# Score products head by head, DFT tables copied later, and a reordered start of each Fourier mixing

## The chip, the cores and the metric

One core of one Trainium2 chip runs the whole program. The metric is device time in microseconds (us), taken as the median of several executions. One execution is also profiled; the instruction rows, waits and granted TensorE clock quoted below come from that one. Five engines work side by side, each through its own queue in order: TensorE (PE, with its weight loads in a row called PEld), VectorE (DVE), ScalarE (ACT), GpSimd (POOL), and SyncE (SP), which only issues transfers.

## The reference

There are two blocks. The first is attention with a threshold, for 8 batches of 8 heads, 576 rows and head dimension 64:

```
scores = scale * q @ k^T
thresh = max(scores, -1) - tau
scores = where(scores >= thresh, scores, -1e9)
attn   = softmax(scores)            # denominator + 1e-9
x      = (attn @ v), heads side by side  -> (8, 576, 512)
```

The second mixes that x and puts it through a channel network:

```
mixed = real(fft over 512 of (fft over 576 of x))
u  = x + mixed
un = (u - mean(u)) / sqrt(var(u) + 1e-6)
out = u + relu(un @ w_ch1) @ w_ch2        # 512 -> 2048 -> 512
```

Everything is fp32; the two weight matrices arrive as float64 and are converted on the chip.

## The kernel before, in words

**Steps.** The attention goes in steps `i`, 20 to a batch (`per_batch`). A pair of heads takes five steps: step `t = i % 5` from 0 to 3 handles 128 query rows of both heads, step 4 the last 64 rows of both together. In a step, `scores` multiplies q by k into two PSUM tiles `sc`, one per head, each 576 wide and made in two halves (L434); the two heads lie on different 64 partitions. The softmax takes the negated maximum (`neg`, L455 in the first two batches, L512 after), the exponentials on ACT (L463, L518) together with a threshold (`thr`), and one DVE instruction that masks and sums (L471, L532). That instruction is the last reader of `sc`. Only two `sc` tiles exist, so the scores of the next step wait for it, head by head. `weights_in_parts` transposes the weights of the step before on PE (`pe` L579, `pw` L597) and copies them out on ACT (`ends` L585, `e_t` L599). `values_in_parts` multiplies them by v (`pv`, L628) and copies the result to `x` (DVE L637 in the first two batches, ACT L635 after). The first pair of a batch goes to a tile called `x_first`. PE results other than scores share four PSUM banks (tag `mm`), handed out in order: a bank is written again only when its last reader is done.

**First batch.** Its 20 steps (`step(i)`) carry, beside attention, the conversion of the first weight matrix in 16 chunks: integer and float passes on DVE (L293, L296, L308), ACT, and POOL (L313, L316). Filler products on PE (`busy`, L111) stand where nothing else is to be done. At the end of step 3 POOL copies the channel DFT table out of the staging tile `dim_raw` (`copy_dim`, 26 instructions), at the end of step 4 the sequence DFT table out of `f` (`copy_seq`), and then clears all of `f` (L228). `fold_rows` adds and subtracts mirrored rows of x into `f`; after the second pair, `fold_halves` (L710, L711) forms sums and differences of two of its chunks on POOL.

**Later batches.** From batch 3 on (`late`) the main loop interleaves one batch's attention with the Fourier mixing and the channel network of rows already mixed. `fill()` sets the interleaving: each call adds a fixed share to a budget, may advance the mixing by one piece (`mix(1)`), and issues channel products until the budget is spent. The first products (`ph`, L1192) and second products (`po`, L1379) use a two-level fast matrix scheme, with sums on DVE and POOL. A mixing begins at step 2 of the following batch (`start_batch`). Its first three pieces are only folds of `f` on DVE (L710, L711, L736, L732, L741). The later ones are products: `py` against the channel table (L751) and `pa` against the sequence table (L768, L772). `Rows.factors` makes the inverse standard deviations: a square root on ACT (L866), an exponential to bring the other function table back (L869), then a DVE reciprocal (L870). `Rows.add` (L877) is what uses them.

Nothing is scheduled by the compiler in this part: each engine executes in the order in which the Python code issues (`manual_schedule`).

Of the kernel before, what the change touches and what calls it, by code (L numbers as in the profile page):

```python
# [9 lines left out]
FP32 = mybir.dt.float32  # L10
# [37 lines left out]
def kernel(  # L48
# [12 lines left out]
    nc = tc.nc  # L61
# [157 lines left out]
    def copy_seq():  # L219
        nc.gpsimd.memset(seq_xe[:, :, :], 0.0)  # L220
        nc.gpsimd.memset(seq_xo[:, :, :], 0.0)
        for u, (pieces, dst, parity, parts) in enumerate(SEQ):
            for p, n in parts:
                for c in range(2):
                    nc.gpsimd.tensor_copy(
                        dst[p : p + n, c, :], f[p : p + n, u, KH * c + parity : KH * (c + 1) : 2]
                    )
        nc.gpsimd.memset(f[:, :, :], 0.0)  # L228

    dim_c = const.tile([128, 1 + 256], FP32, name="dim_c")
    dim_s = const.tile([128, 256], FP32, name="dim_s")

    def load_dim():
        raw = sb.tile([128, DM], FP32, tag="tmp", bufs=1, name="dim_raw")
        nc.sync.dma_start(out=raw[:, :], in_=dft_dim[0:128, :])

        nc.sync.dma_start(out=raw[0:1, EH:DM], in_=dft_dim[128:129, EH:DM])  # L240
        return raw

    def copy_dim(raw):
        nc.gpsimd.memset(dim_s[:, 0:1], 0.0)
        nc.gpsimd.tensor_copy(dim_c[:, 0:1], raw[:, 256:257])
        for u, r in enumerate((0, 2, 1, 3)):
            for n, at in ((32, 0), (1, 32), (31, 33)):
                i = 4 * at + r
                f, step = (i, 4) if i <= 128 else (384 - i, -4)
                c = 64 * u + at  # L250
                nc.gpsimd.tensor_copy(dim_c[:, 1 + c : 1 + c + n], _stepped(raw, f, step, n))

                if f == 0:
                    c, f, n = c + 1, f + step, n - 1
                nc.gpsimd.tensor_copy(dim_s[:, c : c + n], _stepped(raw, 256 + f, step, n))

    w1 = [const.tile([128, HID], FP32, name=f"w1_{c}") for c in range(ND)]
# [12 lines left out]

    hs = const.tile([128, NJ * BT], FP32, name="hs")

# [151 lines left out]
    def scores(i):  # L424
# [5 lines left out]
        if t < 4:  # L430
            for c in range(2):
                for j in range(2):
                    hp, k0 = slice(64 * j, 64 * j + 64), D * (1 - j)
                    nc.tensor.matmul(  # L434
                        sc[j][:, c, 0:HALF], qT[hp, 128 * t : 128 * t + 128],
                        kT[hp, k0 + HALF * c : k0 + HALF * (c + 1)], start=True, stop=True,
                    )
        else:
            for c in range(2):
                nc.tensor.matmul(  # L440
                    sc[0][:, c, 0:HALF], q_ends[:, :], kT[:, D + HALF * c : D + HALF * (c + 1)],
                    start=True, stop=True,
                )
        steps[i] = (sc, nh)

    def softmax(i, between=None, meanwhile=None, behind=None):
# [14 lines left out]
        for j in range(nh):  # L461
# [12 lines left out]
            )  # L474
            if between is not None:
                between()
                between = None
        if behind is not None:
            behind()
        den = inverse(i, nh)  # L480
        if normalized(i // NT):
            nc.vector.tensor_scalar(
# [178 lines left out]
    def fold_rows(n):  # L661
# [39 lines left out]

        if n % NPAIR == 1 and b != 1:
            fold_halves(b)
# [127 lines left out]
    class Rows:  # L831
# [32 lines left out]
        def factors(self):  # L864
# [4 lines left out]
            nc.scalar.activation(out=warm[:, :], in_=eps[:, :], func=ACT.Exp)  # L869
            nc.vector.reciprocal(self.rstd[:, :], self.rstd[:, :])  # L870

        def add(self, t, cols, product):

            u = self.us[t][:, cols]
            if len(product.shape) == 3:
# [591 lines left out]

    def fill(hold=False):
        nonlocal budget, spent
        holding[:] = [True] if hold else []  # L1470
        budget += per_slot
        if mixes and not ended and not hold:
            mix(1)
# [14 lines left out]
    def step(i):  # L1488
# [17 lines left out]
        if t == 1 and n > 0:  # L1506
            softmax(i, lambda: weighted_values(n - 1, 1), next_stages, last_stage)
            load_v(n + 1)
        elif t == 3:
            softmax(i, lambda: weighted_values(n, 0), next_stages, last_stage)  # L1510
        else:
            softmax(i, None, next_stages, last_stage)
# [24 lines left out]
        spread_inverse(i)  # L1537
        if i == 3:
            copy_dim(raw)
        if i == 4:  # L1540
            copy_seq()

    folds = []
# [30 lines left out]
    chunks[3] = w1_chunk(3)  # L1574
    raw = load_dim()
    load_seq()
    load_v(1)
    LAST = HID // WC - 1
# [132 lines left out]
    for i in range(2 * per_batch, total):  # L1711
# [8 lines left out]
        elif t == 1 and n > 0:  # L1720
            while folds:
                fold_more()
            values = values_in_parts(n - 1, 1)
        next(values, None)
        if i < total:
            softmax_first(i)
        next(values, None)
        if i % per_batch == 2:
            for _ in last_fold:
# [34 lines left out]
        if i % per_batch == 1:  # L1764
            next(last_fold)
        fill()
        if t == 2 and n + 1 < B * NPAIR:
# [32 lines left out]
    start_batch(B - 1)  # L1800
    for _ in range(3):
        mix(1)
        fill(True)
# [55 lines left out]
```

## Time and profile before

| what | value |
|---|---|
| median of 3 runs | 1591.63 us (1590.78 to 1592.55) |
| the profiled execution | 1591.6 us, its span 1589.8 us |
| busy in the span | PE 1537.3 us (97%), DVE 1054.1 (66%), ACT 917.1 (58%), POOL 777.3 (49%) |
| mean granted TensorE clock | 0.989 |
| 0 to 134 us (about the first batch) | PE busy 120.6 of 134, DVE 106.5, granted clock 0.95 |
| 134 to 290 us (about the second batch) | PE busy 141.9 of 156, DVE 112.2, granted clock 0.99 |
| 485 to 1305 us (four of the later batches) | PE busy 804.4 of 820 |

A row of the timeline gives the start in us, the duration, engine, line, operation, what it writes and reads, how many instructions were merged in it, and in brackets how long the engine sat idle before it and whose end released it. A row of the waits gives who waited for whom: total us, how often, the longest. A row of the windows gives a stretch, the busy time of each engine in it and the TensorE clock granted there as a share of full speed. PE counts as busy while a matmul is in flight, so a PE at a lower clock still looks busy.

### The profile page before, as it was taken

What the parts mean: (1) busy time and instruction counts of PE and PEld (TensorE: products, weight loads), DVE (VectorE), ACT (ScalarE), POOL (GpSimd) and SP (SyncE); (2) the same over time, 40 slices, a digit from 0 to 9 for tenths busy, and PEclk for the clock granted to TensorE, in tenths of its full rate; (3) what the DMA queues carried; (4) which work ended last, traced back from release to release, by engine and by line L of the source; (5) the groups of instructions that cost most, each with busy time, mean ns of one, the idle gap of its engine ahead of it and who ended that gap; (6) DMA issues with size and microseconds to landing.
All of it is one profiled execution on the core that took longest, in us unless ns stands there. A gap on an engine that the chain in (4) does not pass through costs nothing.

```text
span 1589.8 us, 27001 instructions
## 1 busy us (share of the span) xinstructions
PE 1537.3 (97%) x9786; PEld 1189.8 (75%) x9786; DVE 1054.1 (66%) x2119; ACT 917.1 (58%) x1921; POOL 777.3 (49%) x961
## 2 busy tenths in 40 slices
PE   8989989999999999999999999999999999999999
PEld 4556445555788877877787878877787778889999
DVE  6887776845868566666568466756577666655546
ACT  6775776454665566656766566656666666222231
POOL 4772563034455552546254633545264625546735
PEclk9999999999999999999999999999999999999999
DMA  6423331556956254634445344634464434636655
GB/s 164 128 58 116 76 90 23 168 155 195 318 156 214 70 166 122 205 109 142 141 153 164 116 130 134 203 99 143 125 195 133 137 120 154 213 138 233 237 195 184
DMA packets 248907, 239.31 MB, mean 151 GB/s; under 512 B 197027, under 2 KB 218533, under 8 KB 228678
## 3 DMA queue, kind: packets, MB, share of 16 engines
q1 hardware_dynamic: 246262, 237.28, 48.9%
q8 instruction: 78, 1.28, 0.3%
q10 hardware_dynamic: 2512, 0.30, 0.1%
q14 instruction: 55, 0.45, 0.1%
HBM read 205.93 MB, written 31.46 MB: 149 GB/s over the span
## 4 chain that ended last, share of the span: by engine, by line
PE 81%; DVE 10%; ACT 5%; issue 1%; DMA 1%; POOL 0%; SPq 0%; DVEq 0%; ACTq 0%
PE ph L1192 24%; PE po L1379 17%; PE pv L628 10%; PE sc L434 9%; PE pw L597 7%; PE po L915 4%; PE ph L891 2%; PE sc L440 2%; PE py L751 2%; PE pa L768 1%; DVE neg L455 1%; PE pa L772 1%; PE pe L579 1%; ACT e L518 1%; DVE e L471 1%
## 5 line engine op out<-in xcount | busy, mean ns | idle before, releaser
L512 DVE TENSOR_REDUCE neg<-sc 128x1 f32<-128x576 f32 x216 | 154.3, 751 | 140.0 <-PE sc L434 120.6
L518 ACT ACTIVATE e<-sc,neg 128x576 f32<-128x576 f32 x216 | 158.4, 733 | 144.0 <-DVE neg L512 143.6
L1379 PE MATMUL po<-w,w_all 128*128 128x128 f32 x1728 | 220.9, 278 | 0.3 <-ACT ends L585 0.3
L1379 PEld LDWEIGHTS po<-w,w_all 128*128 128x128 f32 x1728 | 206.6, 193 | 9.8 <-issue 7.1
L1129 DVE TENSOR_TENSOR hs<-ph,hs 128x512 f32<-128x512 f32 (+1 forms) x128 | 105.3, 823 | 160.3 <-PE ph L1192 103.6
L1138 POOL TENSOR_TENSOR w<-hs 128x512 f32<-128x512 f32 x32 | 42.0, 1315 | 317.9 <-ACT hs L1134 244.2
L597 PE MATMUL pw<-ident,e 128*128 128x128 f32 x1152 | 171.4, 276 | 12.6 <-ACT x_first L635 9.0
L1192 PE MATMUL ph<-u_t,w 128*128 128x256 f32 x768 | 180.5, 381 | 0.7 <-DMA w<-f 0.6
L532 DVE SCALAR_TENSOR_TENSOR e<-sc,thr,e 128x576 f32<-128x576 f32 x216 | 168.2, 811 | 18.5 <-ACT thr L522 18.5
L434 PE MATMUL sc<-kT,qT 64*128 64x288 f32 x1024 | 168.9, 432 | 11.3 <-DVE e L471 9.4
L599 ACT COPY e_t<-pw 128x512 f32<-128x512 f32 x256 | 148.6, 594 | 46.0 <-PE pw L597 44.5
L541 ACT ACTIVATE e<-e,den 128x576 f32<-128x576 f32 x216 | 157.6, 776 | 8.3 <-DVE den L385 7.6
L1192 PEld LDWEIGHTS ph<-u_t,w 128*128 128x128 f32 x768 | 141.2, 190 | 23.5 <-issue 4.5
L597 PEld LDWEIGHTS pw<-ident,e 128*128 128x128 f32 x1152 | 135.9, 142 | 30.5 <-ACT x_first L635 10.0
L1192 PE MATMUL ph<-w_all,w 128*128 128x256 f32 x672 | 157.1, 382 | 1.4 <-DVE w_all L1114 1.3
L434 PEld LDWEIGHTS sc<-kT,qT 64*128 64x128 f32 x1024 | 94.1, 187 | 65.2 <-issue 35.1
L1192 PEld LDWEIGHTS ph<-w_all,w 128*128 128x128 f32 x672 | 123.4, 190 | 24.2 <-issue 4.9
L1134 ACT ACTIVATE hs<-hs 128x512 f32<-128x512 f32 (+1 forms) x96 | 74.1, 772 | 113.5 <-DVE hs L1129 112.9
L1244 POOL TENSOR_TENSOR w_all<-w_all 128x128 f32<-128x128 f32 (+2 forms) x160 | 117.0, 747 | 30.3 <-DVE w_all L1399 22.4
L1379 PE MATMUL po<-w,hs 128*128 128x128 f32 x912 | 120.3, 279 | 0.3 <-ACT ends L585 0.3
L1379 PEld LDWEIGHTS po<-w,hs 128*128 128x128 f32 x912 | 110.5, 193 | 9.9 <-issue 7.3
L793 POOL TENSOR_TENSOR u_t<-x,tmp 128x289 f32<-128x289 f32 (+1 forms) x45 | 33.8, 752 | 135.1 <-DVE tmp L788 135.1
(223 smaller groups left out, 2943.8 us busy)
## 6 DMA issues: line engine op xcount, KB each, us to landing
w<-f SPq DMA_DIRECT2D x150, 1024.0 KB, 5.0
hs<-in_moe_w_ch_dram SPq DMA_DIRECT2D x23, 512.0 KB, 4.7
q_in<-in_q_dram SPq DMA_DIRECT2D x128, 72.0 KB, 3.1
out_dram<-u SPq DMA_DIRECT2D x36, 256.0 KB, 2.5
k_in<-in_k_dram SPq DMA_DIRECT2D x124, 72.0 KB, 2.5
v_in<-in_v_dram SPq DMA_DIRECT2D x64, 128.0 KB, 4.7
f<-w SPq DMA_DIRECT2D x14, 512.0 KB, 3.4
f<-w SPq DMA_DIRECT2D x7, 1024.0 KB, 5.1
```

What stands on the lines that cost most here:

```text
L434: nc.tensor.matmul(sc[j][:, c, 0:HALF], qT[hp, 128 * t : 128 * t + 128], kT[hp, k0 + HALF * c : k0 + HALF * (c + 1)], start=True, stop=True,)
L512: nc.vector.tensor_reduce(out=neg[:, j : j + 1], in_=sc[j][:, :, 0:HALF], axis=AXIS_XY, op=ALU.max, negate=True,)
L518: nc.scalar.activation(out=ej, in_=sc[j][:, :, 0:HALF], func=ACT.Exp, bias=neg[:, j : j + 1], scale=1.0)
L532: nc.vector.scalar_tensor_tensor(out=ej, in0=sc[j][:, :, 0:HALF], scalar=thr[:, j : j + 1], in1=ej, op0=ALU.is_ge, op1=ALU.mult, accum_out ...
L541: nc.scalar.activation(out=e[:, S * j : S * (j + 1)], in_=e[:, S * j : S * (j + 1)], func=ACT.Copy, scale=den[:, j : j + 1],)
L597: nc.tensor.transpose(pw[:, c, :], e[:, c0 : c0 + 128], ident[:, :])
L599: nc.scalar.copy(e_t[:, 4 * j : 4 * j + 4, qs], pw[:, :, :])
L628: nc.tensor.matmul(pv[64 * j : 64 * j + 64, 0:m], vt[:, 2 * c + j, :], e_t[:, 4 * j + c, 0:m] if c < 4 else ends[:, 0, 0:m], start=(c == 0 ...
L1129: nc.vector.tensor_tensor(out=to, in0=bank, in1=to if other is None else other, op=ALU.add)
L1192: nc.tensor.matmul(bank[:, 256 * q : 256 * q + 256].rearrange("p (two n) -> p two n", two=2), left[:, 256 * c + 128 * q : 256 * c + 128 * ...
L1244: return lambda: eng.tensor_tensor(out=to, in0=to, in1=other, op=ALU.add)
L1379: nc.tensor.matmul(to, lefts[m][j][:, s], right_[:, 128 * s : 128 * (s + 1)], start=jn in (0, 4) and s == 0, stop=s == 3, skip_group_check ...
```

## The change

Seven edits, in two places of the program.

In the first batch: `scores` issues both halves of one head and then both of the other; `fold_halves` and the copying of the channel table go to the end of the batch (steps 16 to 19), the copying in four parts; `copy_seq` goes from step 4 to step 5; two narrow strips of `f` are cleared in place of all of it; the channel table is loaded to a free part of `hs`. In the first and second head of the softmax, the product of values with the inverse sums (L637) stands behind the second head's masking and the denominators, where it stood between the two heads.

In the later batches: the reciprocal of the deviations is issued at the first `add`; where a mixing begins (step 3), `x_first` is copied ahead of that step's exponentials, and the mixing's third piece of folds comes behind that step's maxima. At the very end the last values are copied out one call earlier, and the loop over the first mixing pieces takes a fourth round that mixes nothing.

```
@@ copy_seq
-        nc.gpsimd.memset(f[:, :, :], 0.0)
+        nc.gpsimd.memset(f[:, :, 145:160], 0.0)
+        nc.gpsimd.memset(f[:, :, FW + 143 : FW + 160], 0.0)
@@ load_dim, copy_dim
-        raw = sb.tile([128, DM], FP32, tag="tmp", bufs=1, name="dim_raw")
+        raw = hs[:, 12 * WC : 13 * WC]
...
+            yield
@@ scores
-            for c in range(2):
-                for j in range(2):
+            order = [(c, j) for c in range(2) for j in range(2)]
+            if i < per_batch:
+                order.sort(key=lambda cj: cj[1])
+            for c, j in order:
@@ softmax
-            if between is not None:
-                between()
-                between = None
+            if between is not None and j == 0:
+                next(between)
...
         den = inverse(i, nh)
+        if between is not None:
+            for _ in between:
+                pass
@@ fold_rows
-        if n % NPAIR == 1 and b != 1:
+        if n % NPAIR == 1 and b > 1:
             fold_halves(b)
@@ Rows.factors, Rows.add
-            nc.vector.reciprocal(self.rstd[:, :], self.rstd[:, :])
+            self.inverted = False
...
+            if not self.inverted:
+                nc.vector.reciprocal(self.rstd[:, :], self.rstd[:, :])
+                self.inverted = True
@@ fill
-        if mixes and not ended and not hold:
+        if mixes and not ended and not hold and not apart:
@@ step
-        if i == 3:
-            copy_dim(raw)
-        if i == 4:
+        if i == 5:
             copy_seq()
+        if i == per_batch - 4:
+            fold_halves(0)
+        if i >= per_batch - 4:
+            next(dim_copies)
@@ main loop of the later batches
         next(values, None)
+        if i % per_batch == 3:
+            next(values, None)
         if i < total:
             softmax_first(i)
         next(values, None)
+        if i % per_batch == 3:
+            mix(1)
...
-        fill()
+        fill(apart=i % per_batch == 2)
@@ behind the main loop
     next(values, None)
+    next(values, None)
     fill(True)
     while held:
         held.pop(0)()
-    next(values, None)
...
-    for _ in range(3):
-        mix(1)
+    for n in range(4):
+        if n < 3:
+            mix(1)
         fill(True)
```

More of the change, by code (lines that the diff above doesn't have):

```diff
@@ L227, in copy_seq @@
                     )
-        nc.gpsimd.memset(f[:, :, :], 0.0)
+        nc.gpsimd.memset(f[:, :, 145:160], 0.0)
+        nc.gpsimd.memset(f[:, :, FW + 143 : FW + 160], 0.0)
+    hs = const.tile([128, NJ * BT], FP32, name="hs")
     dim_c = const.tile([128, 1 + 256], FP32, name="dim_c")
@@ L268 @@
     u_t = const.tile([128, ND, RING], FP32, name="u_t")
-    hs = const.tile([128, NJ * BT], FP32, name="hs")
     shift = const.tile([128, 1], FP32, name="shift")
@@ L430, in scores @@
         if t < 4:
-            for c in range(2):
-                for j in range(2):
+            order = [(c, j) for c in range(2) for j in range(2)]
+            if i < per_batch:
+                order.sort(key=lambda cj: cj[1])
+            for c, j in order:
+                if True:
                     hp, k0 = slice(64 * j, 64 * j + 64), D * (1 - j)
@@ L1466, with fill @@
     held = []
-    def fill(hold=False):
+    def fill(hold=False, apart=False):
         nonlocal budget, spent
@@ L1506, in step @@
         if t == 1 and n > 0:
-            softmax(i, lambda: weighted_values(n - 1, 1), next_stages, last_stage)
+            softmax(i, values_in_parts(n - 1, 1), next_stages, last_stage)
             load_v(n + 1)
         elif t == 3:
-            softmax(i, lambda: weighted_values(n, 0), next_stages, last_stage)
+            softmax(i, values_in_parts(n, 0), next_stages, last_stage)
         else:
@@ L1574 @@
     chunks[3] = w1_chunk(3)
-    raw = load_dim()
     load_seq()
+    dim_copies = copy_dim(load_dim())
     load_v(1)
```

## The prediction

> **What bounds the kernel now.** I read the busy shares first, then the waits of TensorE, then the timeline around the longest of them, then the granted clock there.
>
> ```profile
> PE 1537.3 (97%) x9786; PEld 1189.8 (75%) x9786; DVE 1054.1 (66%) x2119; ACT 917.1 (58%) x1921; POOL 777.3 (49%) x961
> ```
>
> TensorE sets the time: it idles 52 us in 1590. What it computes isn't changed, so a gain can come only from idle time and from time at a lower clock. The waits say where the idle time is:
>
> ```profile
> PE sc L434 <- DVE e L471: 9.4, 8, 3.6
> PE pw L597 <- ACT x_first L635: 9.0, 5, 2.2
> PE pe L579 <- DVE w_all L1399: 4.6, 5, 2.6
> PE py L751 <- DVE f L732: 3.0, 1, 3.0
> ```
>
> The first stands almost wholly in the first batch, the next two at the starts of five mixings (at 513, 688, 863, 1036, 1209 us), the last at the start of the final one (1379 us). One such start, in its order of time:
>
> ```profile
> 500.15 0.18 DVE L870 RECIPROCAL rstd<-rstd 128x4 f32<-128x4 f32 x1 [3.07 <-ACT rstd L866]
> 502.59 1.16 DVE L691 TENSOR_TENSOR f<-x 128x2 f32<-128x2 f32 x1
> 503.75 1.77 DVE L1173 TENSOR_TENSOR w_all<-w_all,hs 128x512 f32<-128x512 f32 x1
> 505.44 0.81 DVE L532 SCALAR_TENSOR_TENSOR e<-sc,thr,e 128x576 f32<-128x576 f32 x1
> 512.40 0.83 PE L751 MATMUL py<-dim_c,f 128*128 128x65 f32 x6
> 513.60 1.41 DVE L512 TENSOR_REDUCE neg<-sc 128x1 f32<-128x576 f32 x2
> 513.82 0.30 PE L579 MATMUL pe<-ident,e 128*128 128x128 f32 x1 [0.59 <-DVE w_all L1399]
> 515.89 0.37 ACT L635 COPY x_first<-pv 128x256 f32<-128x256 f32 x1
> 516.31 0.66 PE L597 MATMUL pw<-ident,e 128*128 128x128 f32 x4 [2.18 <-ACT x_first L635]
> ```
>
> DVE stands still for 3.07 us until ACT's square root is there, and is late from then on: the maxima at 513.6 read scores that were ready at 508.3. ACT holds its copy of `x_first` behind exponentials that need those maxima, so a PSUM bank ready at 510.6 is free only at 516.26, and `pw` waits 2.18 us for it. The clock then falls:
>
> ```profile
> 864.00:866.00 2.00, 0.72 (x5) 0.59 (x6) 2.00 (x2) 1.87 (x7) 0.86 (x1) 0.96 0.75 303
> 866.00:868.00 2.00, 2.00 (x10) 1.67 (x11) 1.93 (x8) 1.28 (x3) 0.00 (x0) 0.50 0.00 0
> 868.00:870.00 2.00, 2.00 (x14) 1.64 (x14) 1.57 (x3) 2.00 (x4) 0.00 (x0) 0.69 0.00 0
> ```
>
> The last three columns are granted clock, DMA share and GB/s. Slices at 0.96, 0.50 and 0.69 lose 2 x (0.04 + 0.50 + 0.31) = 1.7 us. The starts at 513 and 1036 lose 1.7 too, the one at 688 3.4, the one at 1209 nothing. In the first batch:
>
> ```profile
> 39.38 1.75 DVE L293 TENSOR_SCALAR w<-hs 128x512 int32<-128x512 int32 x1
> 43.18 3.00 PE L434 MATMUL sc<-kT,qT 64*128 64x288 f32 x8 [2.35 <-DVE e L471]
> ...
> 99.28 1.24 PE L434 MATMUL sc<-kT,qT 64*128 64x288 f32 x8
> ...
> 102.25 1.69 DVE L296 TENSOR_SCALAR hs<-hs 128x512 int32<-128x512 int32 x1
> 103.86 1.95 DVE L308 SCALAR_TENSOR_TENSOR w<-hs,w 128x512 f32<-128x512 uint32 x1
> 106.69 2.36 PE L434 MATMUL sc<-kT,qT 64*128 64x288 f32 x8 [3.60 <-DVE e L471]
> ```
>
> L293 and L296 take 0.42 us as a rule, L308 0.68. Each slow one here has a POOL instruction over it: at 39.38 the weight product L316, late by the table copies of 32.7 to 37.7; at 102 and 104 the two of `fold_halves`. PE pays with gaps of 2.35 and 3.60 us, and with clocks of 0.50 that lose 3.4 us (43 to 50) and 1.7 us (108 to 111).
>
> **The change, part by part.**
>
> *Channel table later.* POOL loses 5 us of copies at 32.7, so the step-3 weight products come at about 36.3 to 38.9 and are over when L293 starts at 39.38. That instruction is 1.33 us shorter, and what follows in its chain as well: I take 1.5 us of the gap of 2.35. With 0.85 left the clock should hold: 3.4. Together 4.9. The two transfers of the table go behind six of the sequence table on SP; both tables are wanted over 15 us later. The copies now fall on steps 16 to 19, where POOL is idle from 121 to 149 but for them; the first `py` at 139 needs them, and they end by about 130. Without that cover each of the 26 would cost about 0.2.
>
> *`fold_halves` at step 16.* L296 and L308 give back 1.27 + 1.27 = 2.5 us of the gap of 3.60, and the clock 1.7: 4.2. At step 16 POOL has 3.2 us more ahead of the folds of the third pair, DVE has only the last conversion, and the mixing reads the result at 137. Nothing is charged.
>
> *`copy_seq` a step later, strips in place of the whole.* POOL loses the clearing of 2.12 us; the copies (3.7 us) move over another chunk's passes. L296 and L308 took 0.11 more under such copies at 41, L296 1.1 more under a weight product. Between 0 and 3 us lost; I take 1.5, since POOL is crowded there too.
>
> *L637 behind the second masking.* DVE no longer waits there for `pv` (2.4 us in all, 1.7 of it in the clock loss at 113), and the second `sc` tile is free 0.4 us sooner in five steps. `ends` is free about 0.5 us later, behind which ACT has its `e_t` copy and PE the next step's transposes. I take 1.0 gained.
>
> *Head by head.* Today's four products take 1.24 us when nothing holds them, since the heads run side by side on separate rows. After it: a full-height pair of the same width (L440) takes 1.14 us for 4 records, that is about 0.24 each behind a latency of 0.16, so eight in a row take about 1.9 to 2.1. TensorE pays 0.6 in some seven free steps: 4.2. In some nine steps held by the second tile, the first head's two halves no longer stand behind it: DVE's wait of 0.47 to 0.78 before the maxima shortens by about 0.26: 2.4 back. Net 1.5 to 2 lost; I take 1.5. [...] The row decides: L440's four records use one row group, and still follow each other in 0.24 us, with loads of 0.19 hidden. [...]
>
> First batch: 4.9 + 4.2 - 1.5 + 1.0 - 1.5 = 7.1 us.
>
> *Start of a mixing, and the inverse.* Without the wait for ACT, DVE makes the maxima of the step before at 500.4 and not 501.3, and gets L691 and L1173 (1.77, lengthened by POOL) out of the way while ACT, which the square root's table loads hold, makes its exponentials (the first ready with its threshold at 503.0, as now). Masking begins at 503.1 to 503.8, not at 505.44: 1.6 to 2.3 sooner. DVE then does the folds L710, L711, L736, L732 by 508.8, three sums by 510.2, and the maxima 510.2 to 511.6, ahead of the third piece, whose first result is there at 512.1. `py` can start behind the products that end at 512.56, without a gap. `x_first` is out at 511.0, so `pe` and `pw` don't wait: 2.77 us and the clock's 1.7. At 863 and 1036 the rows repeat to within 0.1; at 1209 there is no clock loss. Sum: 3 x (2.7 + 1.7) + 2.7 = 15.9. At 688 I count nothing: there masking is held by exponentials (ACT begins them at 675.9 behind the square root), so DVE gains no lead, the maxima push the third piece to 687.2, and `py` and `pe` wait about 2.8 us in place of `pe`'s 2.62 and `pw`'s 0.24. Behind the moved reciprocal (0.17) wait only the sums of its own rows.
>
> [...] The row above shows half clock behind 2.18 us. [...] I go by the row.
>
> *The end.* The first `py` of the last mixing goes behind 12 products, about 3 us, so it covers the 2.99 us wait for L732; 2.0 counted.
>
> Sum: 7.1 + 15.9 + 2.0 = 25.0 us. The profiled execution took 1591.6 us (span 1589.8, the rest around it), the median 1591.63: the same within 0.1. Predicted 1566.6, a span of 1564.8.
>
> **The rivals.** *A new wait takes the old one's place (0.22).* If DVE is as late as now, the maxima ahead of the third piece hold `py` until 514.2: 1.6 us of gap for 2.77, with the clock still falling. Four starts give 1.1 each, 4.4 for 15.9: 1578. For it: DVE is the late engine at 505 to 513. Against it: the 3.07 us idle.
>
> *The first batch gives nothing (0.12).* The moved POOL work falls on other passes and opens other gaps: 1591.6 - 18 = 1574.
>
> *The start at 688 too (0.10).* A little lead there brings 2.9 + 3.4 and a better first batch: 1559.
>
> *Slower (0.08).* [...]
>
> The likeliest has 0.48, and its own range is 1562 to 1571 (the first batch from 4 to 10, the starts from 14 to 18). Leaving out the slow case and some of the fast one, 1558 to 1582 holds eight in ten; one case of 0.08 alone is slower. Faster by over 0.2% (3.2 us, about what a measurement here can tell from none) 0.89, the same 0.03, slower 0.08.
>
> **What would show it.** The waits of `pw` for `x_first` gone, the reciprocal without idle time before it, no `py` waiting on L732 at four starts, and the clock at 1.00 behind them. In the first batch no gap over 1 us at the seventh and thirteenth steps' scores, L434 eight records in 1.9 to 2.1 us. I am wrong if `py` waits in place of `pw`, or if new slow L293 and L296 stand under `copy_seq`.

## The result, and the profile after

The changed kernel takes 1572.93 us (median of 4 runs, 1570.71 to 1576.82); the kernel before, beside it, 1591.20 us (4 runs, 1589.11 to 1592.55). The ratio is 0.9889, with a 95% interval of 0.9865 to 0.9913: 18.3 us faster, where 25.0 were forecast. The profiled execution took 1571.58 us, its span is 1569.8 us, and the mean granted TensorE clock rose from 0.989 to 0.996.

The busy shares and the waits of TensorE after (waits: total us, how often, the longest):

```profile
PE 1526.0 (97%) x9786; PEld 1187.1 (76%) x9786; DVE 1061.6 (68%) x2119; ACT 916.4 (58%) x1921; POOL 777.5 (50%) x962
```

```profile
PE py L759 <- DVE f L740: 8.8, 5, 2.0
PE sc L440 <- DVE e L477: 4.4, 5, 1.4
...
PE pw L605 <- ACT ends L593: 2.2, 1, 2.2
...
PE py L759 <- DVE w_all L1410: 1.6, 1, 1.6
```

TensorE still sets the time. (After has other line numbers: `sc` L440, masking L540, maxima L520, `pw` L605, `py` L759, the third fold piece L740, the reciprocal L883.) The waits of `pw` for `x_first` and of `pe` for `w_all` are gone, 13.6 us together, and so is the wait of 3.0 us at the end. In their place `py` waits for the third piece of folds, five times, and once for a sum. At the starts of mixings and at the end that makes 16.6 us before and 11.1 after (with 0.7 that `pw` waits at one start). The start that the prediction showed, after the change:

```profile
490.00 1.99 DVE L692 TENSOR_TENSOR f<-half 128x143 f32<-128x143 f32 x2
490.48 2.64 POOL L1161 TENSOR_TENSOR hs<-hs,w 128x512 f32<-128x512 f32 x2
...
497.71 0.16 DVE L883 RECIPROCAL rstd<-rstd 128x4 f32<-128x4 f32 x1
...
498.31 1.87 DVE L718 TENSOR_TENSOR sums<-f 128x608 f32<-128x608 f32 x1
...
503.52 0.37 ACT L643 COPY x_first<-pv 128x256 f32<-128x256 f32 x1 [2.74 <-PE pv L636]
504.28 1.42 DVE L520 TENSOR_REDUCE neg<-sc 128x1 f32<-128x576 f32 x2
505.62 1.74 DVE L740 SCALAR_TENSOR_TENSOR f<-f,factors 128x304 f32<-128x304 f32 x2
506.96 0.49 PE L759 MATMUL py<-dim_c,f 128*128 128x128 f32 x2 [1.17 <-DVE f L740]
507.40 0.60 PE L605 MATMUL pw<-ident,e 128*128 128x128 f32 x4
```

The reciprocal has no idle time before it, `x_first` is out 3.5 us before `pw` needs its bank, and `pw` follows without a gap. But DVE has not become early enough: its third piece, behind the maxima, gives `py` its rows 1.17 us late. The other starts show 1.51 us (677), 2.03 (850), 2.02 (1023), 2.03 (1194) and, at the last, 1.56 (1363).

In the first batch:

```profile
41.24 1.94 PE L440 MATMUL sc<-kT,qT 64*128 64x288 f32 x8 [0.92 <-DVE e L477]
...
82.94 1.08 PE L605 MATMUL pw<-ident,e 128*128 128x128 f32 x4 [2.17 <-ACT ends L593]
...
97.09 1.25 PE L440 MATMUL sc<-kT,qT 64*128 64x288 f32 x8
101.94 1.94 PE L440 MATMUL sc<-kT,qT 64*128 64x288 f32 x8 [1.03 <-DVE e L477]
```

The gaps of 2.35 and 3.60 us are 0.92 and 1.03. One at 83 has grown from 1.10 to 2.17. Eight score products head by head take 1.25 us where nothing holds them, 1.24 before. Their records start in pairs 0.013 us apart (97.092 and 97.105, 97.439 and 97.452), with 0.24 to 0.35 us from pair to pair. Before, when the heads took turns, the pairs were 0.006 to 0.007 us apart.

Where the 20.0 us of the span came from, by the same product in both traces: 6.6 us are gained when the first sine product of the first mixing starts (140.97 before, 134.38 after), 10.3 us at 667, 13.8 us at 736, 14.6 us at 963, 19.9 us at 1380. By cause, 11.1 us of the 20.0 are time lost to a lower clock (18.2 before, 7.1 after, from the table of the experiments) and 8.9 are idle time. The forecast had about 10 of its 25.0 us as clock and 15 as waits.

### The profile page after: what moved, and what is told of

Read it like the earlier page. It is cut to its first block, busy times and chain, and to the rows that moved or that the text cites. A ratio compares the mean times of both kernels' runs of the same rounds, so it can differ in the third digit from the quotient of the medians.

```text
span 1569.8 us, 27001 instructions
## 1 busy us (share of the span) xinstructions
PE 1526.0 (97%) x9786; PEld 1187.1 (76%) x9786; DVE 1061.6 (68%) x2119; ACT 916.4 (58%) x1921; POOL 777.5 (50%) x962
## 4 chain that ended last, share of the span: by engine, by line
PE 83%; DVE 9%; ACT 4%; issue 1%; DMA 1%; POOL 1%; SPq 0%; ACTq 0%; DVEq 0%
PE ph L1203 24%; PE po L1390 18%; PE pv L636 9%; PE sc L440 9%; PE pw L605 7%; PE po L926 4%; PE ph L902 3%; PE sc L446 2%; PE py L759 2%; PE pa L776 1%; PE pe L587 1%; DVE neg L461 1%; PE pn L851 1%; PE pa L780 1%; PE pd L111 1%
## 5 line engine op out<-in xcount | busy, mean ns | idle before, releaser
L520 DVE TENSOR_REDUCE neg<-sc 128x1 f32<-128x576 f32 x216 | 154.3, 751 | 131.4 <-PE sc L440 118.6
L540 DVE SCALAR_TENSOR_TENSOR e<-sc,thr,e 128x576 f32<-128x576 f32 x216 | 168.4, 813 | 19.9 <-ACT thr L530 19.6
L605 PE MATMUL pw<-ident,e 128*128 128x128 f32 x1152 | 169.9, 275 | 5.6 <-ACT ends L593 2.2
L440 PE MATMUL sc<-kT,qT 64*128 64x288 f32 x1024 | 168.1, 431 | 6.6 <-DVE e L477 4.4
L605 PEld LDWEIGHTS pw<-ident,e 128*128 128x128 f32 x1152 | 135.4, 141 | 21.9 <-issue 5.6
L440 PEld LDWEIGHTS sc<-kT,qT 64*128 64x128 f32 x1024 | 95.7, 187 | 57.9 <-issue 26.8
```

The costliest lines, as they stand in the source:

```text
L440: nc.tensor.matmul(sc[j][:, c, 0:HALF], qT[hp, 128 * t : 128 * t + 128], kT[hp, k0 + HALF * c : k0 + HALF * (c + 1)], start=True, stop=True,)
L520: nc.vector.tensor_reduce(out=neg[:, j : j + 1], in_=sc[j][:, :, 0:HALF], axis=AXIS_XY, op=ALU.max, negate=True,)
L540: nc.vector.scalar_tensor_tensor(out=ej, in0=sc[j][:, :, 0:HALF], scalar=thr[:, j : j + 1], in1=ej, op0=ALU.is_ge, op1=ALU.mult, accum_out ...
L605: nc.tensor.transpose(pw[:, c, :], e[:, c0 : c0 + 128], ident[:, :])
```

## The clock, first

The times of one kernel spread over 6 us here, more than some edits are worth, and the reason decides how the experiments are read. Granted clock, slice by slice, in the record of after (columns: stretch; busy us of PE, its loads, DVE, ACT, POOL; the last three are clock, DMA share, GB/s):

```profile
847.63:851.04 3.41, 1.38 (x13) 1.19 (x11) 3.41 (x6) 1.88 (x4) 2.07 (x1) 1.00 0.92 311
851.04:854.45 3.41, 3.30 (x17) 2.36 (x15) 3.34 (x9) 2.49 (x7) 0.00 (x0) 0.50 0.19 74
...
1018.29:1021.70 3.41, 2.47 (x22) 2.31 (x20) 3.41 (x7) 1.13 (x3) 1.38 (x1) 1.00 0.37 72
1021.70:1025.12 3.42, 2.15 (x16) 1.74 (x16) 3.42 (x7) 2.42 (x7) 0.69 (x1) 1.00 0.76 312
1025.12:1028.53 3.41, 3.41 (x28) 3.02 (x28) 3.30 (x9) 2.65 (x6) 1.28 (x1) 1.00 0.03 7
```

The two gaps are alike, 2.03 and 2.02 us. The first lies within one slice, in which PE is idle 3.41 - 1.38 = 2.03 us, and all of the next slice runs at half clock. The second is cut by a slice's edge into 0.94 and 1.27 us (with a little of its surroundings), and nothing is lost. In the granted clock that the profiles of the 14 kernels of this study record, the half-clock stretches of one execution begin on one grid of 3.413 us. There are 73 beginnings in 14 executions (without the stretch in which each execution ends), and within one execution they stand off the grid by 0.03 us at most: before's at 43.23, 108.08 and 517.68 us are 19 and 120 steps apart. The grid's offset is not the same in all executions: it is 1.10 us from the start of the span in after and 2.27 in before. I counted PE's idle time in each slice of the grid that was itself at full clock, from 20 us on, and looked at the clock of the slice behind it:

| idle in a slice of 3.41 us | slices | half clock in the next |
|---|---|---|
| under 0.9 us | 6037 | 0 |
| 0.9 to 1.4 us | 107 | 3 |
| 1.4 to 1.6 us | 58 | 8 |
| 1.6 to 1.8 us | 16 | 3 |
| over 1.8 us | 54 | 53 |

So where over 1.8 us of a slice were idle, about half of it, the next 3.41 us went at half speed in 53 of 54 cases, and 1.7 us were lost. Ten of the 73 stretches last two slices, though the first of the two has only 0.0 to 1.4 us idle: for a slice that is already slow the table does not hold. From the grid and the table I estimate the rest. A gap of 2.03 us leaves 1.7 us or more in one slice if it begins in the slice's first 1.71 us or its last 0.33, some 6 times in 10; otherwise an edge cuts it and, by the table, mostly nothing is lost. Of the two gaps above one cost 1.7 us and the other nothing: by this estimate three such gaps make a kernel's times spread over some 5 us. After's own four runs go with the clock in this way: 1570.71 us at a clock of 0.997, 1571.58 at 0.996, 1574.28 at 0.993, 1576.82 at 0.992. With the lost time estimated from these clocks, the four lose 8.6 us in the mean; 35 runs of the kernel before, made beside the experiments, lose 15.7 (clocks of 0.988 to 0.993). So of the 18.3 us some 7 are clock, and the profiled pair, with 11.1, is a lucky one for the change.

## The experiments

All are the changed kernel with the edit shown; the medians are beside after's 1572.93. The medians are of four runs each, but of five for the later batches undone, ten for `py` later and two without POOL's differences. "Clock lost" is the sum over slices of 2 us of the profiled execution.

| kernel | median, us | range | span | clock lost |
|---|---|---|---|---|
| before | 1591.20 | 1589.11 to 1592.55 | 1589.8 | 18.2 |
| after | 1572.93 | 1570.71 to 1576.82 | 1569.8 | 7.1 |
| first batch undone | 1580.19 | 1578.00 to 1581.42 | 1576.2 | 8.8 |
| later batches and end undone | 1584.03 | 1578.85 to 1585.61 | 1583.7 | 15.6 |
| channel table early | 1575.49 | 1571.62 to 1578.28 | 1573.3 | 11.3 |
| `fold_halves` early | 1578.45 | 1574.64 to 1580.44 | 1578.7 | 15.5 |
| sequence table early, whole clearing | 1576.77 | 1574.77 to 1578.47 | 1576.7 | 12.1 |
| heads by turns | 1573.64 | 1571.17 to 1575.07 | 1572.3 | 10.4 |
| reciprocal early | 1577.30 | 1572.43 to 1579.23 | 1575.7 | 12.8 |
| `x_first` not ahead | 1573.57 | 1570.09 to 1575.17 | 1568.3 | 5.4 |
| third piece ahead of the maxima | 1580.42 | 1575.14 to 1580.51 | 1573.4 | 8.7 |
| third piece split | 1572.47 | 1571.42 to 1574.13 | 1569.6 | 9.8 |
| `py` later | 1584.12 | 1581.66 to 1587.11 | 1579.9 | 11.4 |
| without POOL's differences | 1558.94 | 1557.73 to 1560.16 | 1556.0 | 3.3 |

**The two halves of the change.** `u_first` undoes the edits of the first batch, but for the place to which the channel table is loaded and the order of the transfers:

```
-        nc.gpsimd.memset(f[:, :, 145:160], 0.0)
-        nc.gpsimd.memset(f[:, :, FW + 143 : FW + 160], 0.0)
+        nc.gpsimd.memset(f[:, :, :], 0.0)
-            if i < per_batch:
-                order.sort(key=lambda cj: cj[1])
-                next(between)
+                for _ in between:
+                    pass
-        if n % NPAIR == 1 and b > 1:
+        if n % NPAIR == 1 and b != 1:
-        if i == 5:
+        if i == 4:
-        if i == per_batch - 4:
-            fold_halves(0)
-        if i >= per_batch - 4:
-            next(dim_copies)
+        if i == 3:
+            for _ in dim_copies:
+                pass
```

> All edits of the first batch are undone, those of the later batches stay. Theory (the shortfall of the change lies at the starts of the mixings, the first batch gave what was forecast): the trace after reaches the first product of the first mixing 6.6 us earlier, so this run gives 6 to 8 us back: 1579 to 1581, the clock loss near 50 us is there again, and the starts of the mixings look as in the changed kernel. Rival (part of the first batch's gain was lost again in the second batch): 2 to 4 us back, 1575 to 1577.

Measured: 1580.19 us, 7.3 above after, where the prediction's first batch had 7.1. The half clock near 50 us that was expected did not come; this execution was slow from 103 to 110 us. Nor did the gap of 2.35 us:

```profile
41.36 1.94 PE L437 MATMUL sc<-kT,qT 64*128 64x288 f32 x8 [1.52 <-DVE e L474]
```

`u_later` undoes the edits of the later batches and the end:

```
-            self.inverted = False
+            nc.vector.reciprocal(self.rstd[:, :], self.rstd[:, :])
+            self.inverted = True
-        if i % per_batch == 3:
-            next(values, None)
-        if i % per_batch == 3:
-            mix(1)
-        fill(apart=i % per_batch == 2)
+        fill()
-    next(values, None)
     fill(True)
     while held:
         held.pop(0)()
+    next(values, None)
-    for n in range(4):
-        if n < 3:
-            mix(1)
+    for _ in range(3):
+        mix(1)
```

> All edits of the later batches and of the end are undone, those of the first batch stay. Theory: 11 to 13 us back, 1584 to 1586, with the waits of the transposes for the copy of x_first as before. Rival (most of the gain is the first batch's): under 6 us back, 1579 or less.

Measured: 1584.03 us, 11.1 above after. Its waits are before's:

```profile
PE pw L605 <- ACT x_first L643: 9.1, 5, 2.2
...
PE pe L587 <- DVE w_all L1411: 4.6, 5, 2.6
```

7.3 + 11.1 = 18.4, the 18.3 of the result: the halves add up, as far as medians of runs that spread over 3 to 7 us can show it, and what is missing is missing in the second one, 11.1 where 17.9 were forecast.

**The first batch, edit by edit.** The start of the program differs by up to 1.5 us from one execution to the next (the scores of step `i` = 5 begin at 36.76 us in before, at 36.39 in after and at about 35.4 in `u_dim`), so these are compared by a stretch within it: from the scores of step `i` = 5 to the first sine product of the first mixing. It takes 104.2 us before (36.76 to 140.97), 98.0 after (36.39 to 134.38), and 103.9 with the whole first batch undone. Part of that is the clock, of which the stretch lost 1.7 to 5.1 us:

| kernel | stretch, us | clock lost in it | the rest |
|---|---|---|---|
| before | 104.2 | 5.1 | 99.1 |
| after | 98.0 | 1.7 | 96.3 |
| first batch undone | 103.9 | 3.4 | 100.5 |
| `fold_halves` early | 103.0 | 5.1 | 97.9 |
| channel table early | 98.6 | 1.7 | 96.9 |
| sequence table early, whole clearing | 100.1 | 1.7 | 98.4 |
| heads by turns | 98.0 | 1.7 | 96.3 |

The seven other runs with after's first batch take 96.4 to 99.7 us, and 96.2 to 96.4 without the clock's loss. So the last column tells an edit's worth to some 0.2 us. Before and the first batch undone agree in sum, not in the last column; what makes that difference of 1.4 us was not tested.

`u_halves`:

```
-        if n % NPAIR == 1 and b > 1:
+        if n % NPAIR == 1 and b != 1:
             fold_halves(b)
-        if i == per_batch - 4:
-            fold_halves(0)
```

> The kernel after with the sums and differences of the second pair's rows made in the first batch where they stood before, behind that pair. Theory (worth 4.2 us, 2.5 of the gap at the thirteenth step and 1.7 of clock): the gap near 102 is 3 us or more where it was 1.03, the first product of the first mixing comes near 138, and the time is about 1577. Rival (the gap went for another reason): the gap stays near 1 us, the first product at 134 to 135, 1573.

The stretch takes 103.0 us, 5.0 more, and the median is 5.5 higher. The timeline around it:

```profile
98.13 1.48 POOL L718 TENSOR_TENSOR sums<-f 128x608 f32<-128x608 f32 x1
98.25 1.65 DVE L296 TENSOR_SCALAR w<-hs 128x512 int32<-128x512 int32 x1
...
99.69 1.54 POOL L719 TENSOR_TENSOR f<-f 128x608 f32<-128x608 f32 x1
99.82 1.69 DVE L299 TENSOR_SCALAR hs<-hs 128x512 int32<-128x512 int32 x1
...
102.99 2.99 PE L440 MATMUL sc<-kT,qT 64*128 64x288 f32 x8 [3.54 <-DVE e L477]
```

The two sums on POOL lie on the two conversions, and the gap of 3.54 us and the half clock behind it are back. The mechanism of this step holds. Its size, forecast as 2.5 + 1.7 = 4.2, is 1.6 and 3.4 of clock, since the slow stretch was two slices long in this execution.

`u_dim`:

```
-        if i >= per_batch - 4:
-            next(dim_copies)
+        if i == 3:
+            for _ in dim_copies:
+                pass
```

> The kernel after with all 26 copies of the channel table at the end of step 3 again (its other edits stay). Theory (moving these copies is worth 4.9 us: a gap of about 2.35 us at 43, and lost clock behind it): the first product of the first mixing comes about 4.9 us later than in the kernel after (134.4), near 139, the gap at the scores of the seventh step is again over 2 us where it was 0.92, and the time is about 1578. Rival (the gap went for another reason, such as the later sequence table): the first product at 134 to 136, the gap at or below 1.2 us, 1573 to 1575.

The rival comes much nearer: the stretch takes 98.6 us, 0.6 more than after, the first sine product comes at 134.0, and the gap is

```profile
40.79 1.95 PE L440 MATMUL sc<-kT,qT 64*128 64x288 f32 x8 [1.30 <-DVE e L477]
```

1.30 us for 0.92, a little over the rival's 1.2. The copies alone don't make the gap of 2.35 us that before has there.

`u_seqall`:

```
-        nc.gpsimd.memset(f[:, :, 145:160], 0.0)
-        nc.gpsimd.memset(f[:, :, FW + 143 : FW + 160], 0.0)
+        nc.gpsimd.memset(f[:, :, :], 0.0)
-        if i == 5:
+        if i == 4:
             copy_seq()
```

> The kernel after with the sequence table copied at the end of step 4 and all of f cleared behind it, as before (its other edits stay). From the fifth step's scores to the eighth's the kernel after takes 16.7 us, with all of the first batch's edits undone 20.45, with the channel table's copies alone undone 17.35. Theory (this edit, forecast as a loss of 1.5, is what gained the rest of that stretch, by the clearing of 2.12 us and the weight products that it pushes onto the conversions): the stretch takes 19 to 20.5 us, with gaps of 1.2 to 1.6 at the scores and conversions of 1.5 us or more beside the clearing, and the time is 1575 to 1577. Rival (either step crowds POOL only if both are early): the stretch stays at 16.7 to 17.5, no gap over 1 us there, 1572 to 1574. By the prediction (the edit costs 1.5) it would be 1571.4.

(Steps are counted from 0 in that text: the stretch runs from the scores at 36.39 us of after to those at 53.10.) It takes 18.8 us (35.68 to 54.52) against 16.7, and the longer stretch 100.1, 2.1 more than after; the gaps at its scores are 1.15 and 1.11 us. So the theory's mechanism holds, with the stretch and the gaps just under its ranges:

```profile
41.51 2.13 POOL L228 MEMSET f<- 128x2432 f32 x1
...
43.84 1.50 DVE L298 TENSOR_SCALAR hs<-hs 128x512 int32<-128x512 int32 x1
43.72 1.34 POOL L315 TENSOR_TENSOR w<-w,hs 128x512 f32<-128x512 f32 x1
45.26 1.78 DVE L310 SCALAR_TENSOR_TENSOR w<-hs,w 128x512 f32<-128x512 uint32 x1
```

The clearing pushes the weight products onto L298 and L310, 1.50 and 1.78 us long where 0.42 and 0.68 are usual.

`u_heads`:

```
-            if i < per_batch:
-                order.sort(key=lambda cj: cj[1])
```

> As the changed kernel, but the scores of the first batch alternate between the heads again. By the forecast's term (head by head costs 1.5 us net): 1571.4. Theory from the trace after (eight records head by head take 1.25 us when nothing holds them, as alternating, and VectorE's maxima start sooner): 1 to 3 us slower than the changed kernel, 1574 to 1576.

The stretch takes 98.0 us, as after, and 1573.64 is within after's range: head by head is worth nothing either way, and neither the forecast's 1.5 nor the theory's 1 to 3 came. Undone one by one, the four edits give 1.6 + 0.6 + 2.1 + 0.0 = 4.3 us without the clock, and all together 4.2: they add up. Nothing is left for L637's new place, forecast as 1.0, which was not undone alone. The gap at 83 us is about 2.2 us in every run that has L637 there and 1.1 in the two that don't, and no other edit of the first batch, undone alone, brings 1.1 back. Half clock follows it in 8 of the 12 runs with the longer gap and in neither of the others. So the longer gap most likely comes from L637's place; a run that moves that edit alone would show it.

**The starts of mixings, edit by edit.** `u_rstd` makes the reciprocal behind the square root again:

```
-            self.inverted = False
+            nc.vector.reciprocal(self.rstd[:, :], self.rstd[:, :])
+            self.inverted = True
```

> As the changed kernel, but the reciprocal of the deviations is issued with the square root again. Theory (its lead is mostly eaten before the folds): one or two starts lose up to 2 us, 1573 to 1577. Rival (the step as forecast, a lead of about 2 us at four starts): 6 to 9 us slower, 1579 to 1582.

`py` waits 2.04 us at the first start (1.17 in after), 1.51 at the second as in after, and then

```profile
852.51 0.79 PE L759 MATMUL py<-dim_c,f 128*128 128x128 f32 x2 [1.93 <-DVE f L740]
```

and 1.92 and 1.93 us: no longer than with the moved reciprocal. The idle time before it (2.33 us at 838.57) is back, and the end of the stretch doesn't feel it. Of the 4.4 us in the median 0.9 is the first start and 0.3 the last one; the rest is the clock, of which this execution lost 5.7 us more on gaps that are nearly the same. That is the theory's size without the clock, not the rival's. By that the lead on which the forecast rests never came about at three of the starts.

`u_xfirst`:

```
-        if i % per_batch == 3:
-            next(values, None)
         if i < total:
             softmax_first(i)
```

> The kernel after without the extra round that copies x_first ahead of the exponentials at the start of a mixing. Theory (this copy is the edit that took away the wait of pw, and the wait of py that took its place shares the same stretch): pw waits for x_first again at the five starts, 1.5 to 2.2 us each, behind or beside the wait of py, and the time is 1578 to 1584. Rival (the order of folds and maxima alone makes x_first free in time, since ACT comes earlier): no wait of pw for x_first over 0.5 us, 1572 to 1575.

The rival is right. `pw` doesn't wait for `x_first` (`pe` does once, 0.32 us), `py` waits 8.8 us in five, as in after, and the time is 0.6 from after's. With the third piece behind the maxima ACT has its exponentials early, and the copy behind them is in time without being moved.

`folds_ahead` puts the third piece where it was:

```
-        if i % per_batch == 3:
-            mix(1)
-        fill(apart=i % per_batch == 2)
+        fill()
```

> As the changed kernel, but the mixing's third piece of folds stays where it was, ahead of that step's maxima; x_first is still copied ahead of the exponentials and the reciprocal still at first use. Theory (the new wait of the first mixing products on the folds comes from the maxima standing ahead of them): that wait goes from 8.8 us to under 1.5, and at four or five starts 1 to 2 us are gained, 1564 to 1568. Rival (the folds are late because DVE is late, or the wait only moves to the copies behind the later exponentials): no gain, 1572 to 1577, and the transposes or the sine products wait on ACT instead.

Measured: 1580.42 us, above the theory and the rival. Three of the four runs lie there, at clocks of 0.990 and 0.991; the profiled one took 1575.14 at 0.995. Its waits:

```profile
PE py L759 <- ACT y_e L769: 8.5, 6, 2.0
...
PE pw L605 <- DVE w_all L1410: 2.4, 1, 2.4
```

The cosine products start in time and the sine products wait, 1.93 to 2.00 us at four starts, for a bank that ACT copies out behind its exponentials, which now are late. `folds_split` gives one fold of the piece ahead of the maxima and two behind:

```
+        if late and b < B - 1:
+            yield 0
...
-        fill(apart=i % per_batch == 2)
+        fill()
```

> As the changed kernel, but of the third piece the one fold that the cosine products need goes ahead of the maxima, the other two behind. Theory: the cosine products wait under 0.5 us per start, the sine products up to 0.8, 1566 to 1570. Rival: the wait goes to the sine products in full, 1572 to 1574.

```profile
PE py L761 <- DVE f L751: 8.1, 5, 2.1
```

1572.47 us, as after and as the rival has it: nearly the same wait (1.30 us at the first start, about 2.13 at three), on the sine product. `py_later` leaves the order on DVE and puts the cosine products behind the transposes and eight channel products, the sine products behind the next transposes:

```
-        if mixes:
+        if mixes and i % per_batch != 3:
...
-        fill()
+        fill(apart=i % per_batch == 3)
+        if i % per_batch == 3:
+            mix(1)
...
+        if i % per_batch == 3:
+            mix(1)
```

> As the changed kernel, but where a mixing begins the first cosine products stand behind the transposes of that step and eight channel products, and the sine products behind the second transposes, so that TensorE has 2.9 us of other work while VectorE does maxima and folds. Theory (the 2 us that stay at each start are VectorE's lateness behind the products, whatever stands first in its queue, and can be covered by other work of TensorE): the waits of the mixing products for the folds, 8.8 us, go under 1, with one or two clock losses of 1.7 us: 1562 to 1566. Rival (the wait moves on to the next transposes, whose bank waits for the copies on ScalarE): 1570 to 1574.

```profile
PE py L759 <- DVE w_all L1410: 15.7, 6, 2.9
```

1584.12 us: neither theory nor rival had this size. The first cosine products no longer wait for their rows, but the sine products still do, 0.93 us at three starts, and the cosine products behind those wait up to 2.88 us for a PSUM bank whose reader, a sum on DVE, now comes behind more. Three orders of the same work give three different waiters, and in all of them something of DVE's or behind DVE is late.

**Why DVE is late.** The start near 850, before and then after:

```profile
847.16 0.55 DVE L684 TENSOR_TENSOR f<-half 128x143 f32<-128x143 f32 x2
847.41 2.65 POOL L1150 TENSOR_TENSOR hs<-hs,w 128x512 f32<-128x512 f32 x2
850.03 0.18 DVE L870 RECIPROCAL rstd<-rstd 128x4 f32<-128x4 f32 x1 [2.32 <-ACT rstd L866]
850.13 0.49 DVE L684 TENSOR_TENSOR f<-half 128x143 f32<-128x143 f32 x2
...
854.42 0.80 DVE L532 SCALAR_TENSOR_TENSOR e<-sc,thr,e 128x576 f32<-128x576 f32 x1
...
860.83 0.97 DVE L732 SCALAR_TENSOR_TENSOR f<-f,factors 128x304 f32<-128x304 f32 x2
861.48 0.83 PE L751 MATMUL py<-dim_c,f 128*128 128x65 f32 x6
```

```profile
833.36 3.14 DVE L692 TENSOR_TENSOR f<-half 128x143 f32<-128x143 f32 x4
833.61 2.72 POOL L1161 TENSOR_TENSOR hs<-hs,w 128x512 f32<-128x512 f32 x2
...
838.94 1.77 DVE L1184 TENSOR_TENSOR w_all<-w_all,hs 128x512 f32<-128x512 f32 x1
...
840.63 0.81 DVE L540 SCALAR_TENSOR_TENSOR e<-sc,thr,e 128x576 f32<-128x576 f32 x1
...
847.60 0.56 PE L759 MATMUL py<-dim_c,f 128*128 128x65 f32 x4
847.73 2.07 POOL L1336 TENSOR_TENSOR w_all<-w_all 128x896 f32<-128x896 f32 x1 [4.37 <-DVE w_all L1410]
848.83 1.75 DVE L740 SCALAR_TENSOR_TENSOR f<-f,factors 128x304 f32<-128x304 f32 x2
850.19 0.49 PE L759 MATMUL py<-dim_c,f 128*128 128x128 f32 x2 [2.03 <-DVE f L740]
```

Before, DVE stands still just while POOL makes its two differences L1150, and then the second half of L684 takes 0.49 us. After, the four L692 (L684 of before) lie under the same two differences (L1161) and take 3.14 us, where the four took 0.55 + 0.49 before. The work that moved into the idle time grew by about what the idle time was: masking (L540, before L532) leads the first `py` by 6.97 us after (840.63 to 847.60) and by 7.06 before (854.42 to 861.48). And the third piece, later on DVE, comes under POOL's L1336: 1.75 us for 0.97.

`no_pool_forms` leaves out eight of POOL's differences L1161 in each row group:

```
-        at_slots(1, (1, 2, 4, 6), l1_form(a21, a11, a21, (P, P, P, P)))
-        at_slots(4, (1, 2, 4, 6), l1_form(a12, a12, s1_tile, (P, P, P, P)))
```

> As the changed kernel, but the eight differences of 128 x 512 per row group that GpSimd makes of the left matrices (line 1161 on GpSimd) are left out, so the channel sums are not the reference's. Theory (the lead that VectorE gets from the moved reciprocal is eaten by instructions with two SBUF inputs that GpSimd lengthens): the slow ones on VectorE at the starts (lines 692, 718, 719, 1184 at 1.75 to 2.66 us) fall to their short forms, VectorE is 1.5 to 2 us earlier at the folds, and the waits of the mixing products fall from 8.8 us to under 3: 1564 to 1568. Rival (VectorE is held there by something else): the waits stay at 8 to 9 us, 1571 to 1575.

```profile
828.70 0.99 DVE L692 TENSOR_TENSOR f<-half 128x143 f32<-128x143 f32 x4
...
830.96 1.42 DVE L520 TENSOR_REDUCE neg<-sc 128x1 f32<-128x576 f32 x2 [0.67 <-PE sc L440]
...
842.83 1.11 PE L759 MATMUL py<-dim_c,f 128*128 128x65 f32 x6
```

L692 takes 0.99 us, DVE now waits for the scores at the maxima, `py` runs without a gap at three starts (0.16 and 0.70 us at the other two), and no clock is lost there. The time is 1558.94 us, 14.0 below after and under the theory's range. That is the forecast's picture of these starts, and more is gained than the forecast had, since the differences are gone from everywhere else too. The run shows what makes DVE late, not a faster kernel, and not how much of the 14.0 is the lateness alone. Of the kernels that compute the reference none beats the changed one by more than its spread.

## Why the prediction was right, and where its size was off

The direction and the range (1558 to 1582) hold; of the 25.0 us, 18.3 came. The measured 1572.93 lies outside the likeliest case's own 1562 to 1571, and next to the nearer of the two rivals that expected less (1574 and 1578). The sign "I am wrong if `py` waits in place of `pw`" came true. So the mechanism is right in part: the old waits went as forecast, and a new one took their place.

- *First batch, 7.1.* The sum held (7.3 by the medians), by luck; the terms did not. `fold_halves` at step 16 is worth 5.0 in its run (forecast 4.2), 3.4 of it clock. The channel table later, forecast 4.9, is worth 0.6 with the other edits in place. `copy_seq` a step later with the strips, forecast as a loss of 1.5, gained 2.1. L637's place, forecast as 1.0, leaves nothing to be seen. The failed step is "I take 1.5 us of the gap of 2.35. With 0.85 left the clock should hold: 3.4": it put the whole gap on the copies of 32.7 to 37.7. With these copies early again the gap is 1.30 us, with the sequence copies and the clearing early 1.15, with all of them 1.52, after 0.92. What made the rest of the 2.35 stays open: no run put back the old load order and staging place. Errors of opposite sign met.
- *Head by head.* "Eight in a row take about 1.9 to 2.1" was wrong: 1.25. The spacing of 0.24 us was right, also for products on 64 rows: at 41 us, where the second head is held, the first head's records start at 41.24, 41.56, 41.80 and 42.04. What failed is that it set the second head's records behind the first one's. A second row of four starts there at 41.98, ahead of the first row's last, and where nothing holds the second head the records start in pairs. So the two heads run side by side also when they are issued one after the other. (The trace doesn't name the head of a record; this is read from the starts.) The term of -1.5 measured 0.0. The slower kernel, given 0.08, did not come: head by head took 1572.93 us, by turns 1573.64.
- *The starts, 15.9.* Right: the reciprocal without idle time, the waits of `pw` and `pe` gone. Wrong: "`py` can start behind the products that end at 512.56, without a gap". The step that failed is the one before it, "Masking begins at 503.1 to 503.8, not at 505.44: 1.6 to 2.3 sooner", with durations of the moved work taken from rows in which DVE sat idle under POOL's differences. The folds and sums that moved there were lengthened (L692, at the first start L718 too: 1.87 us for 0.78), so at three starts no lead was left. The first rival is the mechanism that came: the maxima ahead of the third piece hold `py`. It was priced at a gap of 1.6 us, and the gaps are 1.17 to 2.03; its time of 1578 was too high since it kept the clock's loss everywhere.
- *The start at 688*, counted as nothing, gave its share: 2.9 us of waits became 1.51 + 0.70, and the clock's 3.4 us did not come in this execution (half that in five others with the same code there). "The maxima push the third piece" was right there.
- *The end, 2.0.* The wait of 3.0 us became one of 1.56: 1.4.
- *The clock.* Forecast for the starts: 5.1 us gained. The profiled execution lost 8.5 us between 480 and 1380 us before and 1.7 after, but five other executions with the same code there lose 3.4 to 6.8. The mean of the six is 5.1, so 3.4 of the 8.5 is the likelier gain, and the 6.8 of the profiled pair is luck. Going by the row (half clock behind 2.18 us) was right as to the size of gap: half clock followed 53 of the 54 slices with over 1.8 us idle. It missed that the half clock went with the idle time within a slice of the grid, so that an equal gap may cost nothing, as that of 2.02 us at 1023 did.

In sum, of the waits at the starts and the end 12.8 us were to go (four times 2.7 and 2.0) and 5.5 went; the clock's share, forecast at 5.1, was 6.8 in the profiled executions. That is 12.3 against the 11.1 of the medians. With the likelier 3.4 for the clock it is 8.9; both lie within the spread of the runs. The waits are surer: 5.5 for 12.8 is 7.3 too little, about the 6.7 by which the whole change fell short.

## What to carry to other kernels

Idle time of an engine isn't free room for moved work: look at what else runs in just that time (here POOL's differences, under which four L692 took 3.14 us for 1.04), and take the moved instructions' durations from rows that have that company. Where one edit removes a wait, follow the next bank and the next reader before counting it, because the late engine (here DVE) stayed late and another product waited for it (here `py`, 8.8 us in five waits). Where under 1.4 us of a slice of 3.4 us were idle on TensorE, the clock behind it rarely fell here (3 of 107 slices from 0.9 to 1.4 us, none of 6037 below), so shorten a gap that far; shortening 2.2 us to 2.0 only changes the odds, by the estimate above from 6.5 to 6 in 10. Before edits are compared, take the clock's loss off a fixed stretch: here that turned runs 3.3 us apart into runs 0.2 apart.

## What was not expected of the hardware

- In the 14 profiled executions half clock began on a grid of 3.413 us whose offset was not the same in all (1.10 us in after, 2.27 in before), and over 1.8 us of idle time in a slice was enough in 53 of 54 slices.
- Eight fp32 score products of 64 rows by 288 columns took 1.24 us issued by turns (99.28 in before) and 1.25 us issued one head after the other (97.09 in after), with the heads side by side either way, by the starts of the records, and 0.24 us from one record of a head to its next (0.35 from its first to its second); four full-height ones of the same width took 1.14 (64.87 in before).
- POOL's additions and differences over DVE instructions: L296 of 0.42 us took 1.65 (98.25 in `u_halves`), L718 of 0.78 took 1.87 (498.31 in after), four L692 of about 1.0 took 3.14 (833.36 in after), the pair of L740 of 0.97 took 1.75 (848.83 in after). Reductions of scores (L520) and the masking (L540), which read PSUM, took 1.4 (two) and 0.8 us throughout: 216 of L540 took 0.80 to 0.82 in after, 100 of them with POOL at work in a fifth of that time or more.
